# A drain of GpSimd's queue behind expert 6, and the last 128 tokens in two column halves

## The chip, the core and the metric

The kernel runs on one core of a Trainium2 chip. The core has five engines with a queue each: TensorE (PE, with its weight loads as PEld), VectorE (DVE), ScalarE (ACT), GpSimd (POOL) and SyncE (SP). They run side by side and wait for one another on semaphores. Matrix products land in PSUM, and ScalarE and VectorE take them from there to SBUF. SyncE and GpSimd issue DMAs; the indirect ones, which take or put rows by a list of indices, are all GpSimd's. In the profile a "q" behind an engine's name marks what its sequencer does itself: waits, branches, drains. The metric is the device time of one execution in microseconds, and of several executions the median.

## The reference

Windowed causal attention with a linear distance penalty, eight batches, eight heads of 64, 576 positions, followed by a mixture of eight experts with a fixed capacity:

```python
attn = softmax(scale * q @ k.T + bias, masked to 0 <= rel < 128)
x = (attn @ v) as [4608, 512]                 # tokens by heads * width
logits = x @ w_gate                           # [4608, 8]
# pairs (token, expert) in falling order of logit; a pair is taken while the
# token is free and the expert has fewer than 576 tokens
for e in range(8):
    mask = assigned == e                      # 576 tokens each
    h = np.maximum(x[mask] @ w1[e], 0.0)      # 512 -> 1024
    out[mask] = h @ w2[e]                     # 1024 -> 512
```

All is float32 on the outside. The kernel makes the products of the experts from pairs of rounded values (a high and a low part), three products for one.

## The kernel before

The first third of the span is attention, which writes x to DRAM and the logits to SBUF. Then a router finds, expert after expert, the 576 tokens of each (`Router.phase`), and `layer_moe` (called from line 1105, in `moe_attn_kernel`) runs over the eight experts k = 0 to 7 in the order in which the router closes them.

For one expert, `gather` issues five indirect DMAs on GpSimd (line 846; four of 128 rows and one of 64), `turn` transposes the rows on TensorE, `layer1` makes hidden values in eight blocks of 128, and `layer2` makes the output. `layer2` goes over five blocks of tokens t; block 4 has 64 tokens, whose high and low parts stand side by side in 128 columns. Each block takes one PSUM tile `po` of 128 x 512 (a pool of two buffers, `ps_o`), eight steps f over the hidden values with three matmuls each (lines 918, 919 and 921; block 4 has two), a copy to an SBUF tile `o` (a pool of three buffers) on ScalarE (line 929), or on VectorE for block 4 (lines 932 and 933), and one scatter to `out` by an indirect DMA on GpSimd (line 934). For the last expert the order of blocks is 4, 0, 1, 2, 3, and for its block 3 the copy is shared: ScalarE takes columns 0 to 255 (line 926) and VectorE 256 to 511 (line 927). Both write one tile `o`, and the trace shows the second copy behind the first.

Between the steps of `layer1` and `layer2` (their `yield`s) `slot` puts in pieces of the router's next phase, weight loads (SyncE), weight splits (ScalarE and VectorE) and the next expert's gathers. By the last expert none of these is left: GpSimd's queue holds its five scatters alone. A scheduler orders each engine's queue by the order of the program text, with what is ready; GpSimd's queue is served in order.

Behind the loop every engine loads a flag `again` (line 1108) and branches on it (line 1109). It is nonzero where the router's quick search was not exact, and the whole of the second part is then done once more by another search; with these inputs the branch is not taken. The block of the branch that is not taken holds, on GpSimd, waits for the eight counters of its DMAs and an instruction that sets them to what the other branch would have left (INC_SWDGE_SEM). After it come the closing instructions of the program (line 1134): each engine drains its queue and posts to a barrier; GpSimd gathers the posts, releases all, clears the semaphores, and a second barrier ends the program.

Of the kernel before, what the change touches and what calls it, by code (L numbers as in the profile page):

```python
# [5 lines left out]
F32 = mybir.dt.float32  # L6
# [4 lines left out]
ALU = mybir.AluOpType  # L11
# [4 lines left out]
E, DM, F, N = 8, 512, 1024, 4608  # L16
# [800 lines left out]
class MoE:  # L817
# [90 lines left out]
    def layer2(self, w2, h, idx, last=False):  # L908
        nc = self.nc
        hh, hl = h  # L910
        for t in range(5) if not last else (4, 0, 1, 2, 3):
            r = 128 if t < 4 else 64
            po = self.p["ps_o"].tile([128, 512], F32, name="po")
            for f in range(8):
                w = w2[f // 2].rearrange("p a (c d) -> p a c d", c=2)
                wh, wl = w[:, 0, f % 2, :], w[:, 1, f % 2, :]
                a = hh[:, f, 128 * t:128 * t + 128]
                nc.tensor.matmul(po, a, wh, start=(f == 0), stop=False)  # L918
                nc.tensor.matmul(po, a, wl, start=False, stop=(f == 7 and t == 4))  # L919
                if t < 4:  # L920
                    nc.tensor.matmul(po, hl[:, f, 128 * t:128 * t + 128], wh, start=False, stop=(f == 7))  # L921
                if f in (2, 5):
                    yield
            o = self.p["o"].tile([128, DM], F32, name="o")
            if last and t == 3:
                nc.scalar.copy(o[:, 0:256], po[:, 0:256])
                nc.vector.tensor_copy(o[:, 256:512], po[:, 256:512])
            elif t < 4:
                nc.scalar.copy(o, po)  # L929
            else:  # L930
                o2 = self.p["o"].tile([64, DM], F32, name="o2", bufs=1)
                nc.vector.tensor_copy(o2, po[64:128, :])
                nc.vector.tensor_tensor(o[0:64, :], po[0:64, :], o2, ALU.add)
            nc.gpsimd.indirect_dma_start(out=self.out, out_offset=bass.IndirectOffsetOnAxis(ap=idx[:r, t:t + 1], axis=0),  # L934
                                              in_=o[:r, :], in_offset=None)
            yield

# [47 lines left out]
def layer_moe(tc, P, C, r, x, w1, w2, out, exact):  # L985
    m = MoE(tc, P, C, x, w1, w2, out)
    g = m.gather(r.idx[0])
    raw = list(m.loads(r.ei[0], 0, range(SOON)))
    route = (n for k in range(1, E) for n in r.phase(k, exact))
    with tc.issue_after(r.last.ins):  # L990
        for _ in range(EARLY0):
            next(route)
    W = {(0, 0): [m.split(raw[c]) for c in range(HI0)]}
    with tc.issue_after(r.last_pe.ins):
        m.idle = P["ps_h"].tile([128, 512], F32, name="ph")
        m.keep_warm(WARM0)
    tn = m.turn(g, True)
    with tc.issue_after(m.last.ins):
        next(tn)

    with tc.issue_after(m.turned.ins):
        late = P["rt"].tile([1, 1], I32, name="late")
        last = tc.nc.vector.tensor_copy(late, r.ei[0][0:1, 0:1])
    raw += list(m.loads(late, 0, range(SOON, 4)))
    with tc.issue_after(m.last.ins):
        for _ in range(TURN0 - 1):
            next(tn)
    W[0, 0] += [m.split(raw[c]) for c in range(HI0, 4)]
    with tc.issue_after(last.ins):
        for _ in range(EARLY - EARLY0):  # L1010
            next(route)
    for _ in tn:
        pass
    st = dict(wait=0, turn=0)
    raws, loaders = {}, {}

    def slot(k, i):

        st["wait"] -= 1
        if st["wait"] <= 0 and (k + 1 not in r.idx or k + 2 not in r.idx and i >= AHEAD[min(k, 2)]):  # L1020
            st["wait"] = next(route, 0)
        for e, layer, c, due in W_LOAD:
            e += k
            if i >= due and e in r.ei and len(raws.get((e, layer), ())) == c:
                if c == 0:
                    loaders[e, layer] = m.loads(r.ei[e], layer)
                    raws[e, layer], W[e, layer] = [], []
                raws[e, layer].append(next(loaders[e, layer]))
                break
        for e, layer, c, due in W_SPLIT:  # L1030
            e += k
            if i >= due and len(W.get((e, layer), (0,) * 9)) == c and len(raws[e, layer]) > c:
                W[e, layer].append(m.split(raws[e, layer][c]))
                break
        if i >= 16 and k + 1 in r.idx:
            if k not in gathers:
                gathers[k], st["turn"] = m.turn(m.gather(r.idx[k + 1])), i + TURN_WAIT
            elif i >= st["turn"]:
                next(gathers[k], None)
                st["turn"] = i + TURN_STEP  # L1040

    gathers = {}
    for k in range(E):
        i = 0
        for _ in m.layer1(W.pop((k, 0)), m.xg, k == 0):
            slot(k, i)
            i += 1
        for _ in range(9):
            if len(W.get((k, 1), ())) < 4:
                slot(k, i - 1)  # L1050
        for _ in m.layer2(W.pop((k, 1)), m.h, r.idx[k], k == E - 1):
            slot(k, i)
            i += 1
        if k < E - 1:
            while k + 1 not in r.idx:
                next(route)
            while len(W.get((k + 1, 0), ())) < 4:
                slot(k, 31)
            if k not in gathers:
                gathers[k] = m.turn(m.gather(r.idx[k + 1]))  # L1060
            for _ in gathers[k]:
                pass
# [12 lines left out]
def moe_attn_kernel(tc, qk, v, w1, w2, wn, rel, ident, cst, out):  # L1075
    nc = tc.nc
    with ExitStack() as es:
# [25 lines left out]
        for k, b in (("ps_g", 1), ("ps_h", 4), ("ps_o", 2)):  # L1103
            P[k] = es.enter_context(tc.tile_pool(name=k, bufs=b, space=PSUM))
        layer_moe(tc, P, C, r, x, w1, w2, out, False)
        again = P["rs"].tile([1, 1], I32, name="again")
        nc.vector.tensor_copy(again, r.flag[0:1, 0:1])
        go = nc.values_load(again[0:1, 0:1], min_val=0, max_val=1)
        with tc.If(go > 0):
            r.start(True)  # L1110
            layer_moe(tc, P, C, r, x, w1, w2, out, True)
# [26 lines left out]
```

## Time and profile before

| what | us |
|---|---|
| median of three runs (721.76 to 722.57) | 721.82 |
| the profiled execution | 722.27 |
| its span, first to last instruction | 720.5 |
| TensorE busy | 678.5 |
| VectorE busy | 466.9 |
| ScalarE busy | 330.6 |
| GpSimd busy | 155.2 |

The span is that of the profiled execution; what lies between it and the execution's own time is outside the recorded instructions. Register, branch, wait and drain instructions count as no engine's busy time, so the page's parts on busy time and on the chain don't show them: they are read by asking for the instructions of a line. Matmuls are pipelined, so the pace is read from start to start.

### The profile page before, as it was taken

The numbers are of one execution on the slowest core, as the hardware profiler recorded it, in microseconds if no ns is written. First come the engines' busy times: TensorE is split into PE (matmuls) and PEld (weight loads), VectorE is DVE, ScalarE is ACT, GpSimd is POOL, SyncE is SP. The second block draws the span as 40 slices with busy tenths as digits, with TensorE's granted clock in tenths as the row PEclk, the third lists the DMA queues.
The fourth block names the chain that finished last, engine by engine and source line by source line (L and its number), as shares of the span: only waits on it lengthen the run. The fifth ranks groups of instructions, "written<-read, shape, count | busy, mean of one in ns | idle before, by whom it ended". The sixth has DMA issues, their size and how long they took to land.

```text
span 720.5 us, 19162 instructions
## 1 busy us (share of the span) xinstructions
PE 678.5 (94%) x7422; PEld 595.2 (83%) x7423; DVE 466.9 (65%) x1856; ACT 330.6 (46%) x990; POOL 155.2 (22%) x337
## 2 busy tenths in 40 slices
PE   7999999999995699999999999999999999999992
PEld 4898898888884398789789889889988989989981
DVE  5778777877887889779588829828847516414200
ACT  6888888888873253324242233224314314322100
POOL 4021221221220202423141231132132032011010
PEclk9999999999997699999999999999999999999997
DMA  8466465565521443627045234235135235110010
GB/s 293 140 189 192 153 211 184 157 211 166 173 81 52 129 173 117 213 70 269 30 158 180 74 109 155 72 118 176 47 119 170 91 106 174 58 44 23 1 37 34
DMA packets 35140, 92.74 MB, mean 129 GB/s; under 512 B 3808, under 2 KB 13152, under 8 KB 35040
## 3 DMA queue, kind: packets, MB, share of 16 engines
q1 hardware_dynamic: 29152, 72.55, 30.9%
q0 software_dynamic: 5888, 18.88, 8.0%
q8 instruction: 60, 0.98, 0.6%
q14 instruction: 40, 0.33, 0.1%
HBM read 72.54 MB, written 18.87 MB: 127 GB/s over the span
## 4 chain that ended last, share of the span: by engine, by line
PE 80%; DVE 14%; DMA 2%; issue 1%; SPq 0%; ACT 0%; POOL 0%; POOLq 0%; DVEq 0%; ACTq 0%
PE ph L893 28%; PE po L918 10%; PE po L919 10%; PE po L921 8%; PE s L53 6%; DVE u L133 5%; PE pt L53 5%; PE pt L157 4%; PE x L53 3%; PE pg L870 2%; DVE xb L255 2%; PE m L579 1%; DMA craw<-in_cst_dram 1%; DVE PT L165 1%; PE ph L854 1%
## 5 line engine op out<-in xcount | busy, mean ns | idle before, releaser
L893 PE MATMUL ph<-xh,hl 128*128 128x288 f32 (+2 forms) x1024 | 191.7, 299 | 0.0
L893 PEld LDWEIGHTS ph<-xh,hl 128*128 128x128 f32 x1024 | 154.4, 189 | 1.0
L144 ACT ACTIVATE u<-u,mn 128x192 f32<-128x192 f32 (+2 forms) x288 | 123.8, 433 | 23.8 <-DVE mn L133 23.8
L918 PE MATMUL po<-hl,hh 128*128 128x512 f32 x320 | 129.3, 404 | 0.0
L919 PE MATMUL po<-hl,hh 128*128 128x512 f32 x320 | 125.0, 390 | 0.0
L893 PE MATMUL ph<-xl,hl 128*128 128x288 f32 (+2 forms) x512 | 115.7, 296 | 0.0
L899 ACT ACTIVATE hh<-ph 128x288 fp32r<-128x288 f32 (+2 forms) x128 | 46.6, 409 | 146.7 <-PE ph L893 146.6
L133 DVE CUSTOM_DVE_ANT_0 u<-s,bm 128x192 f32<-128x192 f32 x308 | 86.4, 333 | 39.8 <-PE s L53 39.4
L921 PE MATMUL po<-hl,hlo 128*128 128x512 f32 x256 | 100.3, 392 | 0.0
L837 DVE TENSOR_TENSOR hl<-raw,hl 128x512 fp32r<-128x512 f32 x128 | 85.0, 683 | 14.3 <-ACT hl L835 13.9
L934 POOL DMA_INDIRECT out_dram<-o,idx x40 | 45.5, 1138 | 203.9 <-ACT o L929 116.0
L893 PEld LDWEIGHTS ph<-xl,hl 128*128 128x128 f32 x512 | 84.2, 188 | 0.1
L874 DVE TENSOR_TENSOR xl<-pg,xh 128x512 fp32r<-128x512 f32 (+1 forms) x37 | 23.7, 639 | 85.1 <-ACT xh L873 85.0
L904 DVE SCALAR_TENSOR_TENSOR hlo<-ph,hh 128x288 fp32r<-128x288 f32 (+2 forms) x128 | 49.5, 417 | 39.2 <-ACT hh L899 38.8
L835 ACT CAST hl<-raw 128x1024 fp32r<-128x1024 f32 x64 | 65.4, 1048 | 16.3 <-DMA raw<-in_w_dram 11.7
L53 PE MATMUL s<-qk 64*64 64x192 f32 (+1 forms) x1112 | 69.8, 321 | 2.6 <-DVE mn L133 2.3
L918 PEld LDWEIGHTS po<-hl,hh 128*128 128x128 f32 x320 | 60.2, 188 | 11.4
L919 PEld LDWEIGHTS po<-hl,hh 128*128 128x128 f32 x320 | 60.3, 188 | 11.0
L846 POOL DMA_INDIRECT g<-x,idx x40 | 44.8, 1120 | 82.0 <-PE pg L870 33.9
L157 PE MATMUL pt<-ident_sb,u 128*128 128x128 f32 x368 | 53.9, 281 | 7.5 <-DVE PT L165 6.2
L929 ACT COPY o<-po 128x512 f32<-128x512 f32 x31 | 18.2, 587 | 91.3 <-PE po L921 57.3
L921 PEld LDWEIGHTS po<-hl,hlo 128*128 128x128 f32 x256 | 48.0, 188 | 10.6
(219 smaller groups left out, 932.6 us busy)
## 6 DMA issues: line engine op xcount, KB each, us to landing
raw<-in_w_dram SPq DMA_DIRECT2D x64, 512.0 KB, 4.1
qk<-in_qk_dram SPq DMA_DIRECT2D x32, 576.0 KB, 4.8
v<-in_v_dram SPq DMA_DIRECT2D x32, 288.0 KB, 3.7
x<-xb SPq DMA_DIRECT2D x14, 512.0 KB, 3.4
x<-xb SPq DMA_DIRECT2D x8, 128.0 KB, 3.4
x<-xb SPq DMA_DIRECT2D x4, 256.0 KB, 2.3
g<-x,idx POOLq DMA_INDIRECT x40, 3.5
out_dram<-o,idx POOLq DMA_INDIRECT x40, 2.9
```

Of the source, the lines that this page charges most:

```text
L53: put(nc.tensor.matmul(out, w, a, start=start, stop=stop, skip_group_check=True))
L133: put(nc.vector.tensor_tensor_reduce(out=u[rows], in0=x[rows, c:c + 64 * m].rearrange("q (j k) -> q j k", k=64), in1=bm[n % NP][rows, y:y ...
L144: put(nc.scalar.activation(u, u, AF.Exp, bias=st["mn"][:, i:i + 1], scale=-1.0, accum_out=st["sm"][:, i:i + 1]))
L157: put(nc.tensor.transpose(ps[:, c:c + 128], u[:, o + 128 * j:o + 128 * j + 128], ident))
L835: self.last = nc.scalar.copy(hl[:, 0, :], raw)
L837: nc.vector.tensor_tensor(hl[:, 1, c:c + 512], raw[:, c:c + 512], hl[:, 0, c:c + 512].bitcast(F32), ALU.subtract)
L893: nc.tensor.matmul(pp[t], w[:, a, j, fo:fo + 128], x[:, j, cut[t]:cut[t + 1]], start=(j == 0 and a == 0 and x is xh), stop=(j == 3 and a = ...
L899: nc.scalar.activation(o, pp[t], AF.Relu)
L904: nc.vector.scalar_tensor_tensor(d, pp[t][:, c0:c1], 0.0, o[:, c0:c1].bitcast(F32), ALU.max, ALU.subtract)
L918: nc.tensor.matmul(po, a, wh, start=(f == 0), stop=False)
L919: nc.tensor.matmul(po, a, wl, start=False, stop=(f == 7 and t == 4))
L921: nc.tensor.matmul(po, hl[:, f, 128 * t:128 * t + 128], wh, start=False, stop=(f == 7))
```

## The change

It has two parts. In `layer_moe`, behind the last scatter of expert 6 (k == E - 2), GpSimd gets a drain instruction. `layer2` keeps the scatter's handle in `self.sent` for it, and `issue_after` puts the drain behind that scatter in GpSimd's queue. In `layer2`, block 3 of the last expert is made in two halves of 256 columns: each half has a `po` tile of its own, of which it uses its columns alone, 24 matmuls of 256 columns, and a copy by ScalarE. One scatter follows both, as before. The tile `o` is asked for ahead of the matmuls rather than behind them; for all other blocks the loop over halves has one turn of 512 columns.

```diff
--- before.py
+++ after.py
@@ -910,28 +910,28 @@
         hh, hl = h
         for t in range(5) if not last else (4, 0, 1, 2, 3):
             r = 128 if t < 4 else 64
-            po = self.p["ps_o"].tile([128, 512], F32, name="po")
-            for f in range(8):
-                w = w2[f // 2].rearrange("p a (c d) -> p a c d", c=2)
-                wh, wl = w[:, 0, f % 2, :], w[:, 1, f % 2, :]
-                a = hh[:, f, 128 * t:128 * t + 128]
-                nc.tensor.matmul(po, a, wh, start=(f == 0), stop=False)
-                nc.tensor.matmul(po, a, wl, start=False, stop=(f == 7 and t == 4))
+            cols = (slice(0, 256), slice(256, 512)) if last and t == 3 else (slice(0, 512),)
+            o = self.p["o"].tile([128, DM], F32, name="o")
+            for cs in cols:
+                po = self.p["ps_o"].tile([128, 512], F32, name="po")
+                for f in range(8):
+                    w = w2[f // 2].rearrange("p a (c d) -> p a c d", c=2)
+                    wh, wl = w[:, 0, f % 2, cs], w[:, 1, f % 2, cs]
+                    a, out = hh[:, f, 128 * t:128 * t + 128], po[:, cs]
+                    nc.tensor.matmul(out, a, wh, start=(f == 0), stop=False)
+                    nc.tensor.matmul(out, a, wl, start=False, stop=(f == 7 and t == 4))
+                    if t < 4:
+                        nc.tensor.matmul(out, hl[:, f, 128 * t:128 * t + 128], wh, start=False, stop=(f == 7))
+                    if f in (2, 5):
+                        yield
                 if t < 4:
-                    nc.tensor.matmul(po, hl[:, f, 128 * t:128 * t + 128], wh, start=False, stop=(f == 7))
-                if f in (2, 5):
-                    yield
-            o = self.p["o"].tile([128, DM], F32, name="o")
-            if last and t == 3:
-                nc.scalar.copy(o[:, 0:256], po[:, 0:256])
-                nc.vector.tensor_copy(o[:, 256:512], po[:, 256:512])
-            elif t < 4:
-                nc.scalar.copy(o, po)
-            else:
-                o2 = self.p["o"].tile([64, DM], F32, name="o2", bufs=1)
-                nc.vector.tensor_copy(o2, po[64:128, :])
-                nc.vector.tensor_tensor(o[0:64, :], po[0:64, :], o2, ALU.add)
-            nc.gpsimd.indirect_dma_start(out=self.out, out_offset=bass.IndirectOffsetOnAxis(ap=idx[:r, t:t + 1], axis=0),
+                    nc.scalar.copy(o[:, cs], po[:, cs])
+                else:
+                    o2 = self.p["o"].tile([64, DM], F32, name="o2", bufs=1)
+                    nc.vector.tensor_copy(o2, po[64:128, :])
+                    nc.vector.tensor_tensor(o[0:64, :], po[0:64, :], o2, ALU.add)
+            self.sent = nc.gpsimd.indirect_dma_start(out=self.out, out_offset=bass.IndirectOffsetOnAxis(ap=idx[:r, t:t + 1], axis=0),
                                               in_=o[:r, :], in_offset=None)
             yield
@@ -1051,6 +1051,10 @@
         for _ in m.layer2(W.pop((k, 1)), m.h, r.idx[k], k == E - 1):
             slot(k, i)
             i += 1
+        if k == E - 2:
+            with tc.issue_after(m.sent.ins):
+                m.nc.gpsimd.drain()
         if k < E - 1:
             while k + 1 not in r.idx:
                 next(route)
```

On ScalarE, at the end of the last expert, a row of `COPY o<-po` 128x512 is a whole block's copy, and the row of 128x256 is block 3's (the lines behind it are the flag and the branch):

```order
 L899 ACTIVATE hh<-ph 128x288 x16
 L929 COPY o<-po 128x512 x3
-L926 COPY o<-po 128x256
-L1108 TENSOR_LOAD again
-L1109 COMPARE_AND_BRANCH
+L929 COPY o<-po 128x256 x2
+L1112 TENSOR_LOAD again
+L1113 COMPARE_AND_BRANCH
```

ScalarE has two copies of 256 columns where it had one, and nothing else moves on it.

On VectorE, at the same place, the two rows of 64x512 are block 4 of the last expert (`o` and its helper `o2`):

```order
 L904 SCALAR_TENSOR_TENSOR hh<-ph,hh 128x64
-L932 COPY o_10204<-po 64x512
-L933 TENSOR_TENSOR o<-po,o_10204 64x512
-L927 COPY o<-po 128x256
-L1108 TENSOR_LOAD again
-L1109 COMPARE_AND_BRANCH
+L932 COPY o_10205<-po 64x512
+L933 TENSOR_TENSOR o<-po,o_10205 64x512
+L1112 TENSOR_LOAD again
+L1113 COMPARE_AND_BRANCH
```

VectorE loses its copy of 256 columns, so its flag and branch stand directly behind block 4.

On TensorE the last 24 matmuls of 512 columns become 48 of 256, the first 24 for columns 0 to 255; all ahead of them keeps its order. On GpSimd and SyncE all instructions keep theirs; a drain is not among the kinds that this listing shows, and in the built program the new one stands between the fifth scatter of expert 6 and the first of expert 7.

## Rows read from the trace of the kernel before

**Rows 1.** The page: its head, part 1 and the head of part 4.

```profile
span 720.5 us, 19162 instructions
...
PE 678.5 (94%) x7422; PEld 595.2 (83%) x7423; DVE 466.9 (65%) x1856; ACT 330.6 (46%) x990; POOL 155.2 (22%) x337
...
PE 80%; DVE 14%; DMA 2%; issue 1%; SPq 0%; ACT 0%; POOL 0%; POOLq 0%; DVEq 0%; ACTq 0%
```

**Rows 2.** Timeline of all engines at the end; columns: start us, us, engine, instruction.

```profile
706.17 0.39 PE L921 MATMUL po<-hl,hlo 128*128 128x512 f32 x1
706.63 0.37 ACT L926 COPY o<-po 128x256 f32<-128x256 f32 x1 [4.90 <-PE po L921]
707.04 0.42 DVE L927 COPY o<-po 128x256 f32<-128x256 f32 x1 [20.80 <-ACT o L926]
707.74 0.97 POOL L934 DMA_INDIRECT out_dram<-o,idx  x1 [4.76 <-DVE o L927]
```

**Rows 3.** Line 1109: count, duration ns min/median/max, first and last start us.

```profile
L1109 POOLq EVENT_SEMAPHORE  x5: 17/43/43, 708.6 to 711.1; - x5
...
L1109 POOLq INC_SWDGE_SEM  x1: 1788/1788/1788, 711.2 to 711.2; - x1
```

**Rows 4.** Line 1134, the program's closing instructions, from 712 to 714.5 us.

```profile
L1134 SPq EVENT_SEMAPHORE  x12: 28/28/28, 713.0 to 713.6; - x12
L1134 SPq DRAIN  x2: 7/10/13, 713.7 to 713.8; - x2
L1134 POOLq DRAIN  x1: 6612/6612/6612, 713.0 to 713.0; - x1
```

**Rows 5.** Line 1134 over the whole span.

```profile
L1134 POOLq EVENT_SEMAPHORE  x4: 17/17/17, 719.7 to 720.4; - x4
...
L1134 ACTq DRAIN  x2: 8/8/8, 710.6 to 719.9; - x2
L1134 DVEq DRAIN  x2: 10/14/17, 711.0 to 720.0; - x2
```

**Rows 6.** Line 1125, the program's first instructions.

```profile
L1125 POOLq INC_SWDGE_SEM  x1: 27/27/27, 0.1 to 0.1; - x1
...
L1125 POOLq DRAIN  x1: 169/169/169, 0.3 to 0.3; - x1
```

**Rows 7.** Lines 846 (gathers) and 934 (scatters), the latter's time to landing.

```profile
L846 POOL DMA_INDIRECT g<-x,idx x40: 905/966/3262, 243.7 to 598.4; - x40
...
L934 POOL DMA_INDIRECT out_dram<-o,idx x40: 896/1004/2222, 294.8 to 707.7; - x40
...
DMA to landing us min/median/max: 2.6/2.9/7.4
```

**Rows 8.** Timeline of GpSimd; in brackets the idle time before and what ended it.

```profile
519.45 0.85 POOL L765 TENSOR_TENSOR L<-Lt,L 128x288 f32<-128x288 f32 x1
525.85 1.26 POOL L934 DMA_INDIRECT out_dram<-o,idx  x1 [5.56 <-ACT o L929]
...
658.16 0.90 POOL L934 DMA_INDIRECT out_dram<-o,idx  x1 [4.93 <-DVE o L933]
686.52 0.90 POOL L934 DMA_INDIRECT out_dram<-o,idx  x1 [27.46 <-DVE o L933]
```

**Rows 9.** Timeline of ScalarE at the end.

```profile
701.15 0.59 ACT L929 COPY o<-po 128x512 f32<-128x512 f32 x1 [4.85 <-PE po L921]
```

**Rows 10.** Timeline of TensorE: 512 columns at the end, 256 in expert 0.

```profile
701.41 0.39 PE L921 MATMUL po<-hl,hlo 128*128 128x512 f32 x1
...
253.83 0.40 PE L893 MATMUL ph<-xh,hl 128*128 128x256 f32 x2
...
255.87 0.40 PE L893 MATMUL ph<-xh,hl 128*128 128x256 f32 x2
```

**Rows 11.** Stretch by engine (TensorE's granted clock third from last); weight loads, line 893.

```profile
252.00:256.00 4.00, 4.00 (x34) 3.85 (x32) 3.23 (x16) 1.83 (x4) 0.00 (x0) 1.00 0.89 307
...
L893 PEld LDWEIGHTS ph<-xh,hl x128: 186/188/201, 250.7 to 283.5; 128*128 128x128 f32 x128
```

## Prediction, before the run

> **What bounds the kernel now.** I read the page first, then the end of the span engine by engine, then the rows of the instructions that only wait or drain. TensorE is busy for 94% of the 720.5 us, and the chain that ended last is 80% TensorE [rows 1]. But that chain stops at the last scatter, which GpSimd issues from 707.74 to 708.71 [rows 2]; 720.5 - 708.7 = 11.8 us follow in which no engine computes. The reader should see four pieces there. The scatter's data must land: GpSimd's waits for the DMA counters start at 708.6, the last of them at 711.1 [rows 3], so 2.4 us. An instruction named INC_SWDGE_SEM then takes 1.79 us from 711.2 [rows 3]. A DRAIN on GpSimd's queue takes 6.61 us from 713.0 [rows 4]. The closing barrier starts on GpSimd at 719.7 and the span ends at 720.5 [rows 5]: 0.8 us. All other engines have their own drain behind them long before: ACT at 710.6, DVE at 711.0 [rows 5], SyncE at 713.8 [rows 4]. So from 713.8 to 719.7 the program waits for one instruction, the drain.
>
> The same two instructions stand at the program's start too, before any DMA of GpSimd: there INC_SWDGE_SEM takes 27 ns and the drain 169 ns [rows 6]. Between the two drains lie 40 gathers and 40 scatters [rows 7], and no third drain.
>
> **The change, part 1: a drain behind expert 6.** It adds one instruction on GpSimd, behind the fifth scatter of expert 6 (issue 658.16 to 659.06) and ahead of the first scatter of expert 7 (686.52) [rows 8]. It removes none. What it costs where it stands: no row shows a drain in mid-kernel; the ends are 0.17 us [rows 6] and, with 75 of the 80 DMAs behind it, about the 6.61 us of the last one [rows 4], plus up to 7.4 us for the landing of the scatter just issued [rows 7], 14.0 us in all. Behind it on GpSimd is queued the scatter at 686.52 and nothing else, and that waits for VectorE anyway, after 27.46 us of idleness [rows 8]. So I cost it at nothing. If this cover were gone, the late scatter would hold one of three o buffers, which ScalarE's copy at 701.15 [rows 9] needs next, so some 12 us more of slack lie behind the first 27.
>
> What it gives is the question: does the price of the last drain depend on the DMAs issued since the drain before it? Two points of the trace say that the price grows with something: 0.17 us with no DMA behind it, 6.61 us with 80. A straight line through them is (6.61 - 0.17) / 80 = 0.08 us a DMA. It is not the last scatter's own leftover: the drain starts 4.3 us after that scatter's issue ended and 1.9 us after its landing was seen. If a drain settles what lies behind it, the last one has five scatters to settle: 0.17 + 5 x 0.08 = 0.57 us, an estimate from those two rows. The ends are 0.17 and 6.61 us; I take 0.57, nearest to the start's row, since five is nearer to none than to eighty.
>
> The Trainium skill, VectorE: DVE Perf Modes, section The DRAIN you can't avoid, says that the drains of pre- and postamble last a constant 12 ns or so on all five engines. The 6.61 us of rows 4 contradict it for GpSimd. By that page the last drain would have nothing to give and the sum would be part 2 alone.
>
> What is late next: GpSimd would be ready at 713.0 + 0.57 = 713.6, but SyncE runs a row of 12 waits and two drains from 713.0 to 713.8 [rows 4]. Those begin in the tenth in which INC_SWDGE_SEM ends (711.2 + 1.79 = 713.0), so I read them as released by it. The barrier can then start no earlier than 713.8 instead of 719.7. Part 1 gives 719.7 - 713.8 = **5.9 us**, not 6.0.
>
> **Part 2: the last 128 tokens in two column halves.** Before, 24 matmuls of 512 columns fill po, ScalarE copies 256 columns and VectorE the others. After, 24 matmuls of 256 columns, a copy by ScalarE beside the second half, 24 more matmuls of 256, and a second copy by ScalarE; VectorE's copy is gone.
>
> Matmuls: from the one at 701.41 [rows 10] to the last at 706.17 [rows 2] are 21 starts, 4.76 / 21 = 0.227 us each. The 256-column pace is seen in expert 0's first layer: 17 starts between 253.83 and 255.87 [rows 10], 2.04 / 17 = 0.120 us each, at a granted clock of 1.00 [rows 11] and with a weight load before each as here. 48 x 0.120 - 24 x 0.227 = 5.76 - 5.45 = +0.31 us on the path.
>
> Copies: before, the last matmul ends at 706.56, ScalarE's copy runs 706.63 to 707.00, VectorE's 707.04 to 707.46 behind it, the scatter starts at 707.74 [rows 2]. After, only one copy of 256 columns (0.37 us) stands behind the last matmul; VectorE's start-to-end of 0.42 us and the step to it of 0.04 go: -0.46 us. The second half's buffer of po is the one that ScalarE empties at 701.15 + 0.59 [rows 9], the half starts near 703.8: no wait. ScalarE and VectorE leave the program no later than 0.3 us after before, under the 713.8. Part 2 in sum: +0.31 - 0.46 = **-0.15 us**; ends: +0.31 if the step from ScalarE to GpSimd ate the copy's gain, -0.46 if the extra matmul time were nil.
>
> **Sum.** -5.9 - 0.15 = -6.05 us. The profiled execution took 722.27 us for its span of 720.5, so 1.77 lie around the span; 722.27 - 6.05 = 716.2. It was 0.45 above the median of 721.82; taken from the median, **715.8 us**.
>
> **The rivals.**
>
> 1. *INC_SWDGE_SEM shrinks as well.* It costs 27 ns at the start and 1.79 us at the end [rows 3, 6]; if that too comes from what 80 DMAs left, up to 1.76 us more go, and SyncE's row of waits moves up with it. The next bound is then SyncE at about 712.0, still behind ACT and DVE. 721.8 - 6.05 - 1.76 = 714.0. For it: the same pair of points as for the drain. Against: at the end the instruction stands behind the wait for eight counters and may do other work than at the start; one row each can't tell.
>
> 2. *The last drain keeps its price.* Then it pays 6.6 us for being reached at all after GpSimd has worked on DMAs, not for their number, or the work belongs to INC_SWDGE_SEM just before it. The mid drain changes nothing; part 2 alone remains: 721.8 - 0.15 = 721.7, no change. The change then doesn't do what it says. For it: just two drains with a load of any kind, and one price can be a step as well as a line. Against: a fixed price that looks like loading code should show when GpSimd turns from tensor work to DMAs, and the scatter at 525.85, the first after tensor instructions, takes 1.26 us against a median of 1.00 [rows 7, 8]. The Trainium skill, GPSIMD Engine Reference, section 2.1 Instruction dispatch, says that the first call of freshly loaded code pays about 6 us with no instruction of its own in the profile; by it the 6.61 us would be such a load, which the mid drain pays under cover if the code stays (the forecast) or which is paid anew if five scatters push it out (this rival).
>
> 3. *Something in between.* The settled DMAs help, but the rest of the drain is 1.5 to 4.5 us. GpSimd is ready at 714.5 to 717.5 instead of 719.7, so 717 to 719.5 us in all.
>
> 4. *Slower: the last tile falls to the pace of its weight loads.* A weight load takes 188 ns in the records [rows 11]; at 256 columns a matmul (120 ns) no longer covers one if they don't overlap one another. Place: the last 48 matmuls; price: 48 x 0.188 = 9.02 us instead of 5.45, +3.57 - 0.46 = +3.1 us. It decides the sign only if the drain gives back less than 3.1 us; with the drain's price kept, 721.8 + 3.1 = 724.9. Against: expert 0's 256-column matmuls have the same loads and keep 0.120 us.
>
> **How the numbers follow.** Forecast 0.45, rival 1 0.26, rival 3 0.09, rival 2 0.15, rival 4 0.05. A change under 0.2%, 1.4 us, can hardly be told from none here. Faster: 0.45 + 0.26 + 0.09 = 0.80; same 0.15; slower 0.05. The range reaches from rival 1 less the 0.4 us by which single runs differ from the profiled one (713.5) to the top of rival 3 (719.6) and leaves out 0.20. The likeliest case is 715.8.
>
> **What would show it.** Right: GpSimd's closing DRAIN under 0.8 us; a new DRAIN in the 660s, with the scatter near 686.5 unmoved; SyncE's drain the last before the barrier; about 6.0 us between the last scatter's issue and the end of the span instead of 11.8; no copy by VectorE at the end, 48 starts 0.120 us apart, the last scatter 0.15 us earlier. Wrong: a closing DRAIN of 6 us again (rival 2); INC_SWDGE_SEM well under 1.79 us (rival 1); 256-column starts near 0.19 us apart (rival 4).

## The result and the profile after

The changed kernel takes 715.27 us (median of 10 runs, 712.82 to 720.87) against 721.97 us (10 runs, 721.00 to 724.41) for the kernel before on the same chip. The ratio is 0.9915, with a 95% interval of 0.9887 to 0.9943: faster by 0.6 to 1.1%. The forecast was 715.8 us in a range from 713.5 to 719.6. The sum behind it holds two sizes that were wrong in opposite directions; the experiments below tell them apart.

The profiled execution of the changed kernel took 715.13 us for a span of 713.4. Its head stands against [rows 1]:

```profile
span 713.4 us, 19210 instructions
...
PE 679.1 (95%) x7447; PEld 596.6 (84%) x7447; DVE 466.0 (65%) x1855; ACT 331.1 (46%) x991; POOL 154.5 (22%) x337
```

TensorE's work is what it was (679.1 us against 678.5), so the 7.1 us that are missing from the span are no work: nearly all of them are waits at the end, as the five pieces below show. The closing instructions, line 1138 after as 1134 before [rows 4, 5], have these rows (count, duration ns min/median/max, first and last start us):

```profile
L1138 SPq EVENT_SEMAPHORE  x14: 17/28/28, 711.7 to 713.3; - x14
L1138 POOLq EVENT_SEMAPHORE  x4: 17/17/17, 712.6 to 713.2; - x4
L1138 POOLq DRAIN  x3: 46/107/472, 711.8 to 713.1; - x3
L1138 SPq DRAIN  x3: 7/7/13, 712.5 to 712.8; - x3
...
L1138 ACTq DRAIN  x2: 8/8/8, 709.7 to 712.8; - x2
```

GpSimd's closing drain starts at 711.8 and lasts 472 ns where it lasted 6612. That drain ends at 712.28; SyncE's second drain ends at 712.53 and GpSimd's first wait of the barrier starts at 712.56, so what the barrier waited for last is now SyncE's row of waits and drains, not GpSimd. ScalarE's drain stays at 8 ns. The Trainium skill, VectorE: DVE Perf Modes, section The DRAIN you can't avoid, puts such closing drains at some 12 ns on all five engines; the rows of ScalarE and SyncE agree, GpSimd's 6612 and 472 ns don't.

The branch, line 1113 after as 1109 before [rows 3], from 690 to 714 us:

```profile
L1113 POOLq EVENT_SEMAPHORE  x5: 17/43/43, 708.3 to 711.4; - x5
L1113 PEldq COMPARE_BRANCH  x1: 3462/3462/3462, 704.8 to 704.8; - x1
...
L1113 POOLq INC_SWDGE_SEM  x1: 288/288/288, 711.5 to 711.5; - x1
```

INC_SWDGE_SEM takes 288 ns where it took 1788: the forecast had held it unchanged. The last counter's wait starts at 711.4 against 711.1, though the scatter itself was issued earlier. The new drain, by its line:

```profile
L1057 POOLq DRAIN  x1: 7340/7340/7340, 657.5 to 657.5; - x1
```

GpSimd's timeline, in brackets the idle time before and what ended it [rows 2, 8]:

```profile
657.77 0.91 POOL L934 DMA_INDIRECT out_dram<-o,idx  x1 [4.93 <-DVE o L933]
686.13 0.90 POOL L934 DMA_INDIRECT out_dram<-o,idx  x1 [27.45 <-DVE o L933]
...
707.16 0.97 POOL L934 DMA_INDIRECT out_dram<-o,idx  x1 [4.56 <-ACT o L929]
```

The drain's record lies over the scatter at 657.77 and ends at 657.54 + 7.34 = 664.88 (its start to two places, as the trace has it). The scatter behind it comes after 27.45 us of idleness, against 27.46 before, and is still released by VectorE: nobody waited for the drain.

ScalarE at the end [rows 2, 9], and TensorE at the first half's start and twelve matmuls later [rows 10]:

```profile
700.76 0.59 ACT L929 COPY o<-po 128x512 f32<-128x512 f32 x1 [4.85 <-PE po L925]
703.68 0.37 ACT L929 COPY o<-po 128x256 f32<-128x256 f32 x1 [2.33 <-PE po L925]
706.51 0.37 ACT L929 COPY o<-po 128x256 f32<-128x256 f32 x1 [2.46 <-PE po L925]
```

```profile
700.56 0.28 PE L922 MATMUL po<-hl,hh 128*128 128x256 f32 x1
...
702.00 0.28 PE L922 MATMUL po<-hl,hh 128*128 128x256 f32 x1
```

Twelve starts in 1.44 us are 0.120 us each, the pace that was forecast. From the copy of the block before to the last scatter's issue it is 707.16 - 700.76 = 6.40 us; before it was 707.74 - 701.15 = 6.59. The halves bring that scatter 0.19 us forward.

The difference of the two spans then has five pieces. Ahead of that copy 0.39 us (701.15 against 700.76); the same 0.39 stands already at the scatter ahead of the drain (658.16 against 657.77) and still at the one behind it (686.52 against 686.13), so the drain neither brought nor cost any of it. The halves 0.19. From the end of the scatter's issue to the start of INC_SWDGE_SEM, called the landing below, +0.83 (2.52 us before, 3.35 after). INC_SWDGE_SEM -1.50. From its end to the span's end -5.90 (7.48 us before, 1.58 after). The sum is -0.39 - 0.19 + 0.83 - 1.50 - 5.90 = -7.15 us, the difference of the spans, 720.5 and 713.35.

### The profile page after: what moved, and what is told of

Read it like the earlier page. It is cut to its first block, busy times and chain, and to the rows that moved or that the text cites. A ratio compares the mean times of both kernels' runs of the same rounds, so it can differ in the third digit from the quotient of the medians.

```text
span 713.4 us, 19210 instructions
## 1 busy us (share of the span) xinstructions
PE 679.1 (95%) x7447; PEld 596.6 (84%) x7447; DVE 466.0 (65%) x1855; ACT 331.1 (46%) x991; POOL 154.5 (22%) x337
## 4 chain that ended last, share of the span: by engine, by line
PE 76%; DVE 13%; DMA 4%; issue 4%; POOL 1%; SPq 1%; ACT 0%; POOLq 0%; DVEq 0%
PE ph L893 27%; PE po L922 10%; PE po L923 10%; PE po L925 8%; DVE u L133 6%; PE s L53 5%; PE pt L53 4%; PE pt L157 4%; PE x L53 3%; PE pg L870 2%; DVE xb L255 2%; PE m L579 1%; DMA craw<-in_cst_dram 1%; DVE PT L165 1%; DMA g<-x,idx 1%
## 5 line engine op out<-in xcount | busy, mean ns | idle before, releaser
L922 PE MATMUL po<-hl,hh 128*128 128x512 f32 (+1 forms) x328 | 130.7, 399 | 0.0
L923 PE MATMUL po<-hl,hh 128*128 128x512 f32 (+1 forms) x328 | 126.4, 385 | 0.0
L925 PE MATMUL po<-hl,hlo 128*128 128x512 f32 (+1 forms) x264 | 101.7, 385 | 0.0
L922 PEld LDWEIGHTS po<-hl,hh 128*128 128x128 f32 x328 | 61.7, 188 | 11.1
L923 PEld LDWEIGHTS po<-hl,hh 128*128 128x128 f32 x328 | 61.8, 188 | 10.7
L929 ACT COPY o<-po 128x512 f32<-128x512 f32 (+1 forms) x33 | 18.9, 574 | 96.1 <-PE po L925 62.1
L925 PEld LDWEIGHTS po<-hl,hlo 128*128 128x128 f32 x264 | 49.6, 188 | 10.3
```

What stands on the lines that cost most here:

```text
L922: nc.tensor.matmul(out, a, wh, start=(f == 0), stop=False)
L923: nc.tensor.matmul(out, a, wl, start=False, stop=(f == 7 and t == 4))
L925: nc.tensor.matmul(out, hl[:, f, 128 * t:128 * t + 128], wh, start=False, stop=(f == 7))
```

## The experiments

Three questions were open: what the price of a drain and of INC_SWDGE_SEM depends on (the DMAs that GpSimd has issued since the last drain, the rows that they move, or one load of code, called theory C in the expectations); which of the two parts brings the gain; and why the landing got longer (theory F holds TensorE's branch responsible). Each kernel was timed against runs of the kernel before on its own chip: the first four share one (before: 721.84 us), the next four another (723.83), the last three a third (722.11).

**Each part alone.** The first kernel is the one before, with the drain and nothing else:

```diff
+        if k == E - 2:
+            with tc.issue_after(m.sent.ins):
+                m.nc.gpsimd.drain()
```

> The kernel before plus the drain behind expert 6, without the column halves. Theory A (a drain settles the DMAs issued since the drain before it): closing DRAIN of GpSimd near 0.47 us and INC_SWDGE_SEM near 0.29 us as in the changed kernel, VectorE's last copy still there, so the last scatter 0.15 us later than with the halves; about 6 us under the kernel before, near 715.5 to 716. Theory B (the drain's price hangs on something of the last block, not on the earlier drain): closing DRAIN 6.6 us, no gain, 721.9.

Measured: 716.27 us (6 runs), ratio 0.9915, interval 0.989 to 0.994. Its closing drain (line 1137) and its branch (line 1112):

```profile
L1137 POOLq DRAIN  x3: 46/107/472, 711.3 to 712.6; - x3
```

```profile
L1112 POOLq INC_SWDGE_SEM  x1: 288/288/288, 711.0 to 711.0; - x1
```

Both instructions shrink as in the full change, without the halves. The second kernel is the changed one without the drain, the halves alone:

```diff
-        if k == E - 2:
-            with tc.issue_after(m.sent.ins):
-                m.nc.gpsimd.drain()
```

> The column halves without the drain. Both theories of the drain that lay its price on the DMAs or on code: closing DRAIN 6.6 us and INC_SWDGE_SEM 1.79 us as before; last scatter issued 0.15 us earlier behind the last full block's copy, time 721.7, no difference that can be measured. If the halves brought the gain: near 715.5. If the halves bring the wider spread of the changed kernel's runs (712.8 to 720.9 against 721.0 to 724.4), it shows here too; if the drain does, it shows in the run with the drain alone.

Measured: 723.19 us (12 runs), ratio 1.0014, interval 0.9997 to 1.0031: no gain that these runs show. The drain is back at its old price:

```profile
L1134 POOLq DRAIN  x3: 40/107/6612, 713.3 to 720.5; - x3
```

The scatter is issued 0.19 us earlier here too, but its landing takes 3.36 us instead of 2.52. The change itself, run beside these two:

> The changed kernel once more, unchanged, beside the others. Near 715.3 us, closing DRAIN 0.47 us. Its first ten runs spread from 712.8 to 720.9 us with a mean granted clock of 0.974 to 0.976 in the three longest and 0.983 to 0.987 in the others. If the spread belongs to the chip or the day, the kernel before spreads as much beside it; if it belongs to the change, the runs of this one spread by some 8 us again and those of the kernel before by some 3.

Measured: 716.21 us (6 runs), ratio 0.9902, interval 0.9876 to 0.9928; the drain alone lies in the same interval. So the drain brings the gain, and the halves add nothing that these runs can show. Its six runs lie between 713.16 and 718.40 us, the six of the drain alone between 713.68 and 718.65, the twelve of the halves alone between 720.86 and 727.26, and the 23 of the kernel before between 721.30 and 724.84. So the wider spread is not one chip's, and neither part alone is without it; what brings it isn't shown.

**What a drain's price depends on.** The changed kernel with its drain behind expert 0 instead of 6. Then 15 of the 80 DMAs lie ahead of the drain (ten gathers, five scatters) and 65 behind it:

```diff
-        if k == E - 2:
+        if k == 0:
```

> The changed kernel with its drain behind expert 0 instead of expert 6: 15 DMAs stand ahead of it, 65 behind. Theory A, a price per DMA since the last drain (0.08 us each by the line through 0 and 80): closing DRAIN 0.17 + 65 x 0.08 = 5.4 us, INC_SWDGE_SEM 0.03 + 65 x 0.022 = 1.5 us, the drain in the middle 0.17 + 15 x 0.08 = 1.4 us or the landing of the scatter ahead of it (about 3 us), time near 720. Theory C, a price paid once by the first drain that has work to do (code that has to be loaded, for one): the drain in the middle near 6 to 7 us, the closing DRAIN 0.47 us again, time near 715.3.

Measured: 720.57 us (10 runs), ratio 0.9974, interval 0.9962 to 0.9985. The closing drain, and INC_SWDGE_SEM in the row of the branch:

```profile
L1138 POOLq DRAIN  x3: 46/107/5372, 712.5 to 718.4; - x3
```

```profile
L1113 POOLq INC_SWDGE_SEM  x1: 1488/1488/1488, 710.9 to 710.9; - x1
```

The drain in the middle:

```profile
L1057 POOLq DRAIN  x1: 3780/3780/3780, 315.2 to 315.2; - x1
```

It took 3.78 us where theory C asked for 6 to 7. A second drain that still costs 5.37 us is no load of code paid once: theory C falls. The Trainium skill, GPSIMD Engine Reference, section 2.1 Instruction dispatch, states such a load of about 6 us at a first call; no run here shows it at a drain.

To tell the number of DMAs from the rows that they move, 32 small scatters were added to the kernel before: 112 DMAs instead of 80, only 6% more rows. The added scatters write again what was just written:

```diff
+            if t < 4:
+                nc.gpsimd.indirect_dma_start(out=self.out, out_offset=bass.IndirectOffsetOnAxis(ap=idx[:16, t:t + 1], axis=0),
+                                             in_=o[:16, :], in_offset=None)
```

> The kernel before (no drain, no halves) with 32 scatters more: behind each scatter of 128 rows its first 16 rows are scattered once more. 112 DMAs instead of 80, but only 512 rows more on 9216 (6%). If GpSimd's closing DRAIN and INC_SWDGE_SEM are priced per DMA issued: DRAIN 0.06 + 112 x 0.082 = 9.2 us, INC_SWDGE_SEM 0.19 + 112 x 0.020 = 2.43 us. If they are priced per row or descriptor: about 6% more than before, 7.0 and 1.88 us. If the price doesn't depend on what was issued: 6.61 and 1.79 us.

Measured in one execution, 744.76 us (that the added work costs much more than the drain is no matter here). Rows of lines 1137 and 1112:

```profile
L1137 POOLq DRAIN  x3: 40/107/9226, 732.5 to 742.3; - x3
```

```profile
L1112 POOLq INC_SWDGE_SEM  x1: 2428/2428/2428, 730.0 to 730.0; - x1
```

Forty percent more DMAs make the drain 40% longer, with 6% more rows: the price goes by DMAs. By rows it would have been 7.0 us. Next, the changed kernel with a drain behind each of the first seven experts, to see whether several drains add up or collide:

```diff
-        if k == E - 2:
+        if k < E - 1:
```

> The changed kernel with a drain behind each of the experts 0 to 6 instead of behind 6 alone. If a drain settles the DMAs since the last drain only, those in the middle stand behind 15, 15, 10, 10, 10, 10 and 5 DMAs and cost 0.5 to 1.3 us or, where the scatter just issued lands later, some 3 us, all under waits of GpSimd; closing DRAIN 0.47 us, INC_SWDGE_SEM 0.29 us, time as the changed kernel, 715 to 716.5. If each drain settles all DMAs since the start, the seventh costs 7.3 us again and the closing one 6.6. If a drain holds up gathers or scatters that somebody waits for, it is slower than the change by what it holds.

Measured: 716.12 us (4 runs), ratio 0.9897, interval 0.9874 to 0.992. The seven drains, and the closing one:

```profile
L1057 POOLq DRAIN  x7: 3085/6007/8432, 314.3 to 658.4; - x7
```

```profile
L1138 POOLq DRAIN  x3: 46/107/462, 713.1 to 714.4; - x3
```

The end is as cheap as with one drain. The seven in the middle were longer than expected (0.5 to 3 us); their records hold the wait for the scatter ahead of them and its landing, and each ends 0.6 to 1.1 us behind the last packet of that scatter. The time shows none of it: its ratio lies within the interval of the kernel with one drain.

Last, the drain as late as it can stand, behind the last but one scatter, so that a single DMA follows it:

```diff
+            if last and t == 2:
+                with self.tc.issue_after(self.sent.ins):
+                    nc.gpsimd.drain()
```

> The changed kernel with its drain behind the last but one scatter of the last expert, so that 79 DMAs stand ahead and one behind. The drain starts near 702.6 and needs 0.06 + 79 x 0.082 = 6.5 us, until 709.1, while the last scatter would be issued at 707.16: by the price per DMA the last scatter is held for 2 us, the closing DRAIN falls to 0.15 us and INC_SWDGE_SEM to 0.19 + 0.02 = 0.21 us, which give back 0.08 on the path: 1.9 us slower than the change, near 717. If the price were paid once and for all early, or the drain ran beside the next scatter: the last scatter unmoved, the time that of the change or 0.1 less.

Measured: 719.4 us (6 runs), ratio 0.9936, interval 0.9917 to 0.9955: 3.3 us behind the kernel with seven drains beside it (716.12), and 4.4 us ahead of the kernel before. The drain by its line, the scatters ahead of it and behind it, and the closing drain:

```profile
L938 POOLq DRAIN  x1: 7732/7732/7732, 705.3 to 705.3; - x1
```

```profile
705.57 0.97 POOL L934 DMA_INDIRECT out_dram<-o,idx  x1 [4.47 <-ACT o L929]
714.17 0.97 POOL L934 DMA_INDIRECT out_dram<-o,idx  x1 [7.63 <-ACTq L1112]
```

```profile
L1137 POOLq DRAIN  x3: 46/107/145, 717.2 to 718.5; - x3
```

The closing drain is down to 145 ns and INC_SWDGE_SEM to 203, but the drain in the middle has no cover left: it ends at 713.07 and the last scatter starts at 714.17, where its data would have let it start near 711.1 (5.54 us behind the scatter before it, the step in the changed kernel's own trace). The bracket names ScalarE's branch as the releaser; ScalarE's last copy had ended at 710.83, and the wait that was left is the drain. It was expected to hold the scatter for 2 us. Its end is 1.96 us late, as expected; then another 1.10 us pass before the scatter starts, and no row shows what fills them. Of the 3.06 us of lateness 1.97 come back: from the end of the scatter's issue to the end of the span it is 3.65 us here and 5.62 in the kernel with seven drains, for the landing is shorter too. So the two traces put 1.1 of the 3.3 us down to the drain. They differ by 2.85 us more at the first gather (244.72 us against 241.87), ahead of any drain; how much of that is in the medians isn't shown.

The closing drains of these kernels fall on one line:

| DMAs of GpSimd since the last drain | closing drain, ns | INC_SWDGE_SEM, ns |
|---|---|---|
| 1 | 145 | 203 |
| 5 | 472 | 288 |
| 65 | 5372 | 1488 |
| 80 | 6612 | 1788 |
| 112 | 9226 | 2428 |

From 5 to 65 DMAs the drain grows by 4900 ns, 82 ns a DMA, and a constant of 64 is left; at 80 that makes 6.62 us and at 112 9.25. INC_SWDGE_SEM grows by 20 ns a DMA with 188 left, exactly so in the last four rows. What it does in that time no row shows. The pair at the program's start, 169 and 27 ns with no DMA [rows 6], lies on neither line. With many DMAs ahead of it the drain in the middle follows the same line, counted from the end of the issue just before it: in the changed kernel 664.88 - 658.68 = 6.20 us with 75 DMAs ahead of it (64 + 75 x 82 = 6214 ns), in the last experiment 713.07 - 706.54 = 6.53 us with 79 (6542 ns).

**Why the landing got longer.** In the traces TensorE's sequencer reaches the branch before its last matmul starts (702.9 against 706.17 [rows 2]), and the record of the branch lasts several microseconds. Before, on line 1109:

```profile
L1109 PEldq COMPARE_BRANCH  x1: 4032/4032/4032, 702.9 to 702.9; - x1
```

It ends at 707.0, 0.4 us behind the end of the last matmul; in the changed kernel it starts at 704.8, ends at 708.2, 1.75 us behind the last matmul, and 1.0 us later an instruction packet of 16 KB moves on queue q8. With the halves this packet falls on the last scatter's data. DMA queues of the changed kernel from 708.6 to 711 us (packets, MB, share of 16 engines):

```profile
q0 software_dynamic: 80, 0.26, 31.1%
q8 instruction: 1, 0.02, 2.7%
q14 instruction: 2, 0.02, 2.5%
```

With the drain alone, the packets that start between 708.9 and 710.5 us are all the scatter's (one packet on q14 that started just before runs until 709.50):

```profile
q0 software_dynamic: 80, 0.26, 45.7%
```

To test it, flag, branch and second pass were left out of the changed kernel and of the kernel with the drain alone (the inputs here never take that pass):

```diff
-        again = P["rs"].tile([1, 1], I32, name="again")
-        nc.vector.tensor_copy(again, r.flag[0:1, 0:1])
-        go = nc.values_load(again[0:1, 0:1], min_val=0, max_val=1)
-        with tc.If(go > 0):
-            r.start(True)
-            layer_moe(tc, P, C, r, x, w1, w2, out, True)
```

> The changed kernel without the branch behind the last expert: the flag's load, the compare and the second pass, which isn't taken with these inputs, are left out. In the traces so far the last scatter's counters need 1.9 to 4.3 us from the end of its issue with the column halves and 2.5 us without, and TensorE's branch ends at 707.8 to 709.6 with the halves and 706.8 to 707.0 without, followed by a fetch of 16 KB by the instruction queue that lies on the last scatter's packets. Theory F (that fetch delays the landing): without the branch the landing takes 1.9 to 2.0 us, the tail shrinks by INC_SWDGE_SEM and up to 2.4 us of landing, time near 713 or less, and the runs spread less. Theory G (the landing varies by itself): 2 to 4 us again, with the same spread of runs.

> The kernel before with the drain behind expert 6, without the column halves and without the branch, the flag's load and the second pass (not taken with these inputs). Beside the same kernel with the halves it shows what the halves are worth where no fetch of the branch's code can lie on the last scatter. By the sum of the prediction the halves give 0.15 us: from the last full block's copy by ScalarE to the start of the last scatter 6.30 us here against 6.15 with them, then the same landing (data moving for 0.8 us) and a time 0.15 us above that kernel's 714.3. If the halves cost something else too, this one is the faster of the two by more than 0.3 us in the tail.

Measured: with the halves 714.31 us (4 runs), ratio 0.9877, interval 0.9852 to 0.9901; without them 713.1 us (5 runs), 0.9876, 0.9856 to 0.9896. In both the last scatter's data takes 0.83 us, and from the end of its issue to the end of the span it is 3.19 us. The closing drains of GpSimd and TensorE without the branch, with the halves and without:

```profile
L1132 POOLq DRAIN  x3: 51/107/3202, 707.9 to 712.0; - x3
...
L1132 PEldq DRAIN  x2: 13/1179/2345, 705.2 to 711.8; - x2
```

```profile
L1131 POOLq DRAIN  x3: 51/107/3196, 709.6 to 713.7; - x3
...
L1131 PEldq DRAIN  x2: 13/2140/4267, 704.4 to 713.5; - x2
```

GpSimd's 3.2 us are mostly the landing, not the price: the drain now stands directly behind the scatter, and it ends 0.59 us behind the scatter's last packet (with the halves the issue ends at 709.12, the data at 710.52, the drain at 711.11). TensorE's drain, where the branch stood, lasts 2.3 and 4.3 us and ends 0.05 us behind the last matmul: much of such a record is matmuls that are still to run.

So without the branch the data isn't held up. The halves then keep what was forecast for them: from the copy of the block before to the last scatter it is 6.40 us with them and 6.59 without, and the end behind it is the same. These 0.19 us are far below what the runs can tell, and the two ratios are as good as equal. The 713 us or less that theory F asked for were not reached with the halves. How the data and TensorE's fetch lie to each other in the other traces (from the start of the first to the end of the last packet):

| kernel | last scatter's data, us | fetch on q8, us | data took | landing |
|---|---|---|---|---|
| before | 709.28 to 710.67 | 707.68 to 708.67 | 1.39 | 2.52 |
| drain alone | 708.99 to 710.41 | 707.45 to 708.52 | 1.42 | 2.56 |
| drain behind expert 0 | 709.57 to 710.45 | 710.44 to 711.63 | 0.88 | 1.94 |
| halves alone | 708.67 to 710.89 | 709.20 to 710.21 | 2.22 | 3.36 |
| changed kernel | 708.70 to 710.91 | 709.22 to 710.24 | 2.21 | 3.35 |
| changed, again | 708.34 to 711.45 | 708.52 to 710.41 | 3.11 | 4.26 |
| drain behind each expert | 709.60 to 712.21 | 709.79 to 711.25 | 2.61 | 3.75 |
| drain ahead of the last scatter | 715.71 to 716.55 | 712.85 to 714.16 | 0.84 | 1.87 |
| drain, one copy (below) | 710.98 to 712.23 | 709.76 to 711.17 | 1.25 | 2.33 |
| changed, a third time (below) | 712.41 to 713.62 | 713.39 to 714.40 | 1.21 | 2.25 |
| no branch, with or without halves | - | none | 0.83 | - |

Where the fetch lies within the data, the data takes 2.2 to 3.1 us; where it lies ahead or behind, or meets it for 0.2 us at most (the last two), 0.8 to 1.4. Six of these traces have the halves, the branch and no drain among the last scatters. In four of them the fetch falls on the data; in two it comes behind or at its end, and there the branch's record is longer (3.9 and 3.8 us against 3.4 to 3.5). The landings of the six are 3.15 us on average, those of the three kernels without halves 2.47.

The fetch on q8 isn't alone. In every trace of the table 71 to 80 of the scatter's 80 packets have ended 0.85 us after the first one started; what lasts longer is the few that are left, six in the changed kernel. And in every trace in which the data takes more than 0.84 us, instruction packets of 8 KB on queue q14 lie on it too: 709.15 to 709.81 in the kernel before, 708.90 to 709.50 with the drain alone, 709.18 to 709.72 and 710.21 to 710.63 in the changed kernel. In the three kernels at 0.83 and 0.84 us neither queue moves a packet beside the data. So the 0.4 to 0.6 us between 0.8 and 1.4 go with q14, and the longer times with both queues. As no trace has q8 within the data and q14 away, and the kernels without the branch take both away, what q8 costs by itself isn't shown, nor why such a packet holds a few of the scatter's back for so long.

**A simpler second part.** The drain, and one copy of 512 columns by ScalarE in place of the two shared ones, with no halves:

```diff
-            if last and t == 3:
-                nc.scalar.copy(o[:, 0:256], po[:, 0:256])
-                nc.vector.tensor_copy(o[:, 256:512], po[:, 256:512])
-            elif t < 4:
+            if t < 4:
                 nc.scalar.copy(o, po)
```

> The drain behind expert 6, no column halves, and the last block's 512 columns copied by ScalarE in one instruction, as for the other blocks, instead of 256 by ScalarE and then 256 by VectorE. A copy of 512 columns takes 0.59 us in the traces, the two of 256 in a row 0.83. From the last matmul's end to the scatter 0.08 + 0.59 + 0.27 = 0.94 us, against 1.18 before and 0.73 + 0.31 of more matmul time with the halves: the scatter 0.24 us earlier than before and 0.1 earlier than with the halves. TensorE's branch then ends near 707.0 as before, ahead of the scatter's packets, so the landing takes 2.5 us instead of 3.3 to 4.3: by that 0.9 us or more faster than the change. If the landing's length has nothing to do with the branch's code: 0.1 us faster, not to be told from it.

> The changed kernel once more, for the comparison with the single copy on one chip. TensorE's branch ends 2 us or so behind the last matmul's start and its fetch lies on the last scatter's packets: landing over 3 us. Time near 716.

Measured: 714.83 us (6 runs), ratio 0.9894, interval 0.9877 to 0.9912, and the changed kernel beside it 717.11 us (6 runs), ratio 0.9908, interval 0.9885 to 0.9931. The last copy and the last scatter of the kernel with one copy:

```profile
708.58 0.59 ACT L926 COPY o<-po 128x512 f32<-128x512 f32 x1 [4.89 <-PE po L921]
```

```profile
709.44 0.97 POOL L931 DMA_INDIRECT out_dram<-o,idx  x1 [4.51 <-ACT o L926]
```

The copy of the block before starts at 703.10, so the scatter comes 709.44 - 703.10 = 6.34 us behind it: 0.25 us earlier than with the shared copy and 0.06 earlier than with the halves. One copy of 0.59 us is shorter than two of 0.37 and 0.42 in a row, and it needs no second set of matmuls. The intervals of the two kernels overlap, so it isn't shown to be faster than the change; no run shows it slower, and it has less code. The 0.9 us that were expected of a shorter landing could not show here: in the changed kernel's trace beside it the fetch came behind the data, and the landing was 2.25 us, not over 3.

## Why the prediction was right, and where its sum was not

**The drain.** Right in mechanism and size: 0.472 us measured for 0.57 forecast, from a line through two points, 0.08 us a DMA there and 0.082 in the runs. The 0.1 us too much is the line's start: 0.17 us was taken from the program's first drain, and the runs leave 0.064. The rival in which the drain keeps its price and the one in between have fallen: with 5 DMAs the price is that of 5.

**The cover in mid-kernel.** Right. The drain took 7.34 us, inside the bounds of 0.17 and 14.0, under an idle time of 27.45 us that did not move. The kernel with the drain ahead of the last scatter shows what the same drain does where the cover is too short: the last scatter starts 3 us late.

**SyncE is late next.** Right. Its last drain ahead of the barrier ends at 712.53, behind GpSimd's drain, which ends at 711.81 + 0.47 = 712.28. From the end of INC_SWDGE_SEM to the end of the span the change gave back 5.90 us; the forecast was 5.9.

**INC_SWDGE_SEM: the mis-sized term.** The sum held it at 1.79 us; it fell to 0.288. That is rival 1's mechanism, to which the prediction gave 0.26, and 1.50 of the 1.76 us that it allowed. Its argument against, that at the end the instruction stands behind a wait for eight counters and may do other work, was a guess; the same two rows that made the line of the drain gave one for this instruction too, (1.79 - 0.03) / 80 = 0.022 us a DMA, and it was the same evidence. The runs give 0.020.

**The halves.** Right on the path that was costed: 0.120 us a matmul, and -0.19 us to the scatter's issue for -0.15 forecast. The weight loads' pace, rival 4, didn't come. Wrong in what was left out: the prediction took the landing of the last scatter as given and asked of ScalarE and VectorE alone when they leave the program, not of TensorE's sequencer. With 48 short matmuls instead of 24 it reaches the branch later, 704.8 for 702.9, and its fetch falls on the data, together with packets of q14: +0.83 us in the profiled execution, though not in every one, as the table shows. The part costed at -0.15 us has shown no gain, ratio 1.0014 alone (0.9997 to 1.0031).

**The sum.** Forecast -5.9 - 0.15 = -6.05; measured in the traces -5.90 - 1.50 + 0.83 - 0.19 = -6.76, and 0.39 more from ahead of both parts of the change. The medians differ by 721.97 - 715.27 = 6.70. So the time was met within 0.5 us with the right chief cause, and with two errors, 1.50 and 0.83 us, of which one hid half of the other: the size of the chief term was foreseen, the closeness of the total is luck. The interval of the measured gain reaches from 4.1 to 8.2 us, so the time alone could not have told the sum from one with other terms. By its own sign, about 6.0 us from the last scatter's issue to the end of the span, 5.22 were measured; that sign, not the time, shows the mis-sized term. Rival 3's time has a slip at its lower end: with GpSimd ready at 714.5 its own sum gives 716.5 us, not 717; no chance hangs on it.

## What to carry to other kernels

Ask what the closing drain of a queue costs: where GpSimd has issued many DMAs, put one drain into an idle stretch of its queue that is longer than the drain, as late as such a stretch is to be found; a drain that the last transfer has to wait for gives back part of what it saves. Where a price has two points in the profile, at no load and at full load, every instruction that has the same two points deserves the same line through them. When work is cut finer at the end of a program, follow every engine to its last instruction, not only those on the path: a branch that comes later can bring its fetch onto the last transfer.

## What the runs showed of the hardware

GpSimd's closing drain cost 64 ns and 82 ns for each DMA that GpSimd had issued since the drain before (1 to 112 of them), whether the DMA moved 16 rows or 128; INC_SWDGE_SEM cost 188 ns and 20 for each. A drain that stands right behind a scatter also waits for its landing: with 5 to 15 DMAs ahead of it, it ended 0.6 to 1.1 us after the scatter's last packet; with 75 or 79 ahead of it, 6.2 and 6.5 us from the end of the last issue, the landing lies inside its price.

The branch past the second pass stood in TensorE's sequencer for 3.4 to 4.2 us where ScalarE's took 50 ns, in part beside the last matmuls: it ended 0.2 to 0.5 us behind the last of them with 512 columns, and 1.7 to 2.2 us with 256. Where the instruction packets of q8 and q14 lay on a scatter's data, the data took 2.2 to 3.1 us; with those of q14 alone, or with q8 meeting it for 0.2 us, up to 1.4; with neither, 0.83 to 0.84.

TensorE's granted clock near the start differs from trace to trace. It is the third number from the end in these stretches of the changed kernel, from the trace beside the one copy (span 716.0 us) and from the first (713.4 us):

```profile
12.00:16.00 4.00, 3.13 (x33) 2.13 (x33) 1.94 (x9) 4.00 (x18) 1.86 (x10) 0.62 0.97 340
16.00:20.00 4.00, 3.10 (x24) 2.41 (x25) 2.14 (x17) 1.88 (x9) 0.50 (x3) 0.50 0.44 164
20.00:24.00 4.00, 4.00 (x69) 3.67 (x71) 2.52 (x12) 3.08 (x12) 0.00 (x0) 0.60 0.48 147
```

```profile
12.00:16.00 4.00, 2.32 (x39) 1.66 (x41) 2.91 (x16) 4.00 (x19) 1.88 (x10) 1.00 0.99 364
16.00:20.00 4.00, 4.00 (x86) 3.52 (x89) 2.75 (x15) 4.00 (x19) 0.41 (x3) 1.00 0.79 268
20.00:24.00 4.00, 3.54 (x81) 3.04 (x72) 3.47 (x25) 3.65 (x15) 0.23 (x1) 1.00 0.39 104
```

In the first the clock falls to its lower level, 1.2 GHz (0.50), after a stretch from 8 to 12 us with 42 matmuls at full clock that the second has too, and the first gather comes at 245.85 us instead of 242.40, 3.45 us later. From 16 to 20 us it is 0.50 in three of the thirteen traces (with the drain ahead of the last scatter, with one copy, and here), whose first gathers come at 244.63 to 245.85 us, and 1.00 in the ten others, whose first gathers come at 241.87 to 243.69. What brings it is open. It lies ahead of everything that the change touches, so a difference between two whole spans can hold it.
